# Two alternating chains of exponential steps on VectorE, with 72 instead of 67 tiles

## The chip, the cores and the metric

The kernel runs on one core of one Trainium2 chip. The metric is the device time of one execution in microseconds. Each time is the median of several executions; the profile is of one execution.

## The reference

Attention with a soft cap over 8 batches and 12 heads, 448 tokens, head size 64, and behind it a soft mixture of 8 experts with 4 slots each:

```python
scores = scale * np.matmul(q, k.transpose(0, 1, 3, 2))
scores = cap * np.tanh(scores / cap)                 # cap = 30
scores = scores - np.max(scores, axis=-1, keepdims=True)
attn = np.exp(scores)
attn = attn / (np.sum(attn, axis=-1, keepdims=True) + 1e-09)
x = np.matmul(attn, v)                               # heads side by side: (3584, 768)

logits = x @ phi                                     # (3584, 32)
d = softmax over tokens of logits; slot_input = d.T @ x
slot_out[e] = np.maximum(slot_input[e] @ w1[e], 0.0) @ w2[e]
c = softmax over slots of logits; out = c @ slot_out
```

## The kernel before

The 96 heads are taken as 48 pairs. A pair's scores stand transposed, keys on the partitions: a *tile* is 64 keys of each of the two heads on 128 partitions, with 448 queries along the free axis, so a pair has 7 tiles and the whole work 336. Six tiles make a *chunk*; there are 56 chunks, and the main loop's iteration `j` works on chunk `j`. The loop's pattern repeats every seven iterations: 42 tiles, six pairs, the twelve heads of one batch.

For each half chunk (three tiles) TensorE writes scores to one of two PSUM buffers `sc` (`qk_chunk`, line 316), and ScalarE takes tanh into the chunk's buffer `ex` as f16 (`tanh_chunk`, line 325). The exponential of `cap` times that is then made in place, as bf16. For most tiles ScalarE does it (`exp_chunk`, line 329, one instruction a chunk). The first `taken(j)` tiles of some chunks go to VectorE instead, where `poly_exp` makes the exponential in eight steps: a power of two by scaling into the exponent's bits and a polynomial of the third degree for the rest. Steps 0, 1, 2, 4 and 7 (lines 369, 371, 372, 374 and 377) have one tensor as input; steps 3, 5 and 6 (lines 373, 375, 376) have two. Steps 1 to 6 use the work buffers `xf` and `xp`; steps 0, 6 and 7 write into the tile itself. There is one `xf` and one `xp`, each two tiles wide, so a chain of a chunk has to be past step 6 before the next chain's step 1.

Two iterations after a pair's last tile was scored, TensorE multiplies its seven tiles by the values (`pv_first`, `pv_tail`, `pv_rest`, line 395) into the one PSUM buffer `pv`; VectorE then takes the reciprocal of the sums (line 402) and scales (line 405). VectorE also copies transposed keys, queries and outputs out of PSUM (`kT` and `qT` at line 278, `xT` at line 457). GpSimd casts the values of the next pairs to bf16 (`vcast`, line 286, behind the PV that used the buffer), copies the small exponentials `e` of the mixture (line 488, after ScalarE made them at line 482), and issues the DMAs that load queries and keys (line 186) and the experts' weights (lines 117 and 121). SyncE issues the loads of the values.

The order on each engine is written out by hand (`manual_schedule`): an instruction stands where Python issues it. An iteration runs named slots in a fixed order, `0`, `m`, `e`, `a`, `b`, `r`, `c`, `d`, each with a part `<` ahead and a part `>` behind, and side work is put into them with `at(j, slot, ...)`. Between them stand the tanh of both halves (ahead of `m` and `e`), the exponential of chunk `j - 1` and the first part of PV (between `e` and `a`), the scores of the next chunk (ahead of `b`, and between `c` and `d`), and the rest of PV with its reciprocal and scaling (between `b` and `c`).

Which chunks VectorE takes tiles of, and where each of the eight steps stands, are the tables `SHARE` (by `j % 7`: chunk's tiles, then for each step the distance in iterations and the slot) and `EDGE` (for the first and last chunks). After the attention come the last pairs, the experts' two layers (lines 845 and 878) and the outputs (lines 914, 918, 961, 968, 970).

Of the kernel before, what the change touches and what calls it, by code (L numbers as in the profile page):

```python
# [12 lines left out]
U16 = mybir.dt.uint16  # L13
F16 = mybir.dt.float16
# [4 lines left out]
P = 128  # L19
# [3 lines left out]
S = 448  # L23
# [14 lines left out]
def kernel(  # L38
# [27 lines left out]
    NCH = NTILE // CH  # L66
# [66 lines left out]

    att = ExitStack()
    ld = att.enter_context(tc.tile_pool(name="ld", bufs=1))
    NP = 2
    homes = {}
    for nm in ("qk0", "ex1", "wk", "ldv", "ex2", "ex3", "vb0", "qk1", "ex4", "ex0", "vb1"):
        homes[nm] = att.enter_context(tc.tile_pool(name=nm, bufs=1))
# [1 line left out]
    vb = [homes["vb0"], homes["vb1"]]  # L141
    qk = [homes["qk0"], homes["qk1"]]
    ldv, wk = homes["ldv"], homes["wk"]
    xf = wk.tile([P, NP * S], U16, name="xf")
    xp = wk.tile([P, NP * S], F16, name="xp")
    xs = att.enter_context(tc.tile_pool(name="xs", bufs=4))
    attp = ExitStack()
    psS = attp.enter_context(tc.tile_pool(name="psS", bufs=2, space=PSUM))
    psV = attp.enter_context(tc.tile_pool(name="psV", bufs=1, space=PSUM))
# [181 lines left out]
    def exp_chunk(j):  # L331
# [1 line left out]

    SHARE = {0: (2, ((0, "<b"), (0, ">d"), (1, ">a"), (1, ">a"), (1, ">b"), (1, ">d"), (1, ">d"), (2, ">a"))),
# [4 lines left out]
    EDGE = {3: (1, ((0, ">b"), (0, ">b"), (0, "<c"), (0, ">c"), (0, ">d"), (1, ">a"), (1, ">a"), (1, "<b"))),  # L341
# [7 lines left out]
    shared = {j: SHARE[j % 7] for j in range(3, NCH - 2)  # L349
              if j % 7 in SHARE and j + SHARE[j % 7][1][-1][0] < NCH - 1}  # L350
    shared.update(EDGE)

    octaves = cap * math.log2(math.e)
    base = math.ceil(octaves) + 1
    if base + octaves > 127:
        shared = {}

    def taken(j):
        return shared[j][0] if j in shared else 0
# [4 lines left out]
    def poly_exp(j, tiles, n):  # L364
        n1 = tiles * S
        t = exs[j][:, 0:tiles, :].rearrange("p u s -> p (u s)")
        y, f, p = t.bitcast(U16), xf[:, 0:n1], xp[:, 0:n1]
        steps = (
            lambda: dve.tensor_scalar(y, t.bitcast(F16), octaves * STEP, base * STEP + c0,  # L369
                                      ALU.mult, ALU.add),  # L370
            lambda: dve.tensor_scalar(f, y, STEP - 1, None, ALU.bitwise_and),  # L371
            lambda: dve.tensor_scalar(p, f, c3, c2, ALU.mult, ALU.add),  # L372
            lambda: dve.tensor_tensor(p, p, f, op=ALU.mult),  # L373
            lambda: dve.tensor_scalar(p, p, c1, None, ALU.add),  # L374
            lambda: dve.tensor_tensor(p, p, f, op=ALU.mult),  # L375
            lambda: dve.tensor_tensor(y, y, p, op=ALU.add),  # L376
            lambda: dve.tensor_scalar(y, y, 128.0 / STEP, 128.0 * (127 - base),
                                      ALU.mult, ALU.add))
        steps[n]()
# [173 lines left out]
    def at(j, slot, f, *a):  # L553
        if j < 0:
            j, slot = 0, "b"
        aux.setdefault((j, slot), []).append((f, a))
# [21 lines left out]
    for b in range(B):  # L578
        j, p = b * PER, 6 * b

        def when(nm):
            return j + WHEN[nm][0], WHEN[nm][1]
# [17 lines left out]
        if b < B - 1:  # L600
# [5 lines left out]
                at(*when("en"), e_norm, b)  # L606
            if b % 2:
                at(*when("es"), e_sums, b // 2)
    for j, (tiles, places) in shared.items():
        for n, (dj, slot) in enumerate(places):  # L610
            at(j + dj, slot, poly_exp, j, tiles, n)
    for n, job in enumerate(wjobs):
        at(1 + n * (NCH - 5) // len(wjobs), "b", *job)
    for j, slot, n in ((0, "a", 10), (0, "c", 10), (1, "b", 10), (1, "c", 8)):
# [207 lines left out]
    for n0, half in sorted(w2_spilled, key=lambda x: (x[1], x[0])):  # L822
        t = tl.tile([P, 4, HD], BF16, name=f"w2t{n0}_{half}")
# [123 lines left out]
    for n in range(B // 2 * NT):  # L947
        bb, c = divmod(n, NT)
# [15 lines left out]
        if n == NH or c == 0 or full:  # L964
            ob, n1 = wts.tile([P, 2, 2, HD], F32, name="ob", tag="w1", bufs=E), n
# [44 lines left out]
```

## Time and profile before

| | |
|---|---|
| median of 3 runs | 296.27 us (295.21 to 296.57) |
| span of the profiled execution | 293.9 us, first to last instruction |
| mean granted TensorE clock | 0.985 |
| time of the profiled execution itself | not given; by the three runs 1.3 to 2.7 us lie outside the span |
| exponential on ScalarE (line 329) | 58 instructions, 119.5 us busy |
| tanh on ScalarE (line 325) | 113 instructions, 147.5 us busy |
| steps of `poly_exp` on VectorE | 28 chains of two tiles, 11 of one; 312 of VectorE's 554 instructions |

Engines: PE is TensorE's matmul, PEld its weight load, DVE VectorE, ACT ScalarE, POOL GpSimd, SP SyncE. A line of a timeline gives the start and the duration in us, the engine, the line of the kernel, the operation, the output and input tiles with their shapes, and how many instructions it stands for; in brackets the idle time ahead and what ended it. A busy engine isn't an engine at its best: an instruction that is held by another engine counts as busy, and neighbours that don't depend on each other overlap a little, so that the time from one start to the next is what an instruction costs.

### The profile page before, as it was taken

What the parts mean: (1) busy time and instruction counts of PE and PEld (TensorE: products, weight loads), DVE (VectorE), ACT (ScalarE), POOL (GpSimd) and SP (SyncE); (2) the same over time, 40 slices, a digit from 0 to 9 for tenths busy, and PEclk for the clock granted to TensorE, in tenths of its full rate; (3) what the DMA queues carried; (4) which work ended last, traced back from release to release, by engine and by line L of the source; (5) the groups of instructions that cost most, each with busy time, mean ns of one, the idle gap of its engine ahead of it and who ended that gap; (6) DMA issues with size and microseconds to landing.
All of it is one profiled execution on the core that took longest, in us unless ns stands there. A gap on an engine that the chain in (4) does not pass through costs nothing.

```text
span 293.9 us, 10870 instructions
## 1 busy us (share of the span) xinstructions
PE 255.4 (87%) x4728; PEld 173.9 (59%) x4728; DVE 240.4 (82%) x554; ACT 260.3 (89%) x211; POOL 138.2 (47%) x200
## 2 busy tenths in 40 slices
PE   8898889998999899979988998899989899998620
PEld 6655556756675667556756675667566668542300
DVE  3728998999999999999999989999999976246740
ACT  4999999999999999999999999999999997237620
POOL 4593554763676367635673658365643220300000
PEclk9999999999999999999999999999999999999985
DMA  7999999999999999999999999999999567989896
GB/s 273 217 194 206 221 176 212 203 191 218 230 218 193 210 228 224 199 208 227 189 179 217 223 217 184 216 229 228 209 191 219 131 216 237 407 321 376 323 427 287
DMA packets 58561, 68.13 MB, mean 232 GB/s; under 512 B 4241, under 2 KB 54673, under 8 KB 58513
## 3 DMA queue, kind: packets, MB, share of 16 engines
q0 software_dynamic: 42448, 35.31, 77.8%
q1 hardware_dynamic: 15776, 31.89, 30.8%
q8 instruction: 37, 0.61, 0.8%
q10 hardware_dynamic: 288, 0.23, 0.2%
q14 instruction: 12, 0.09, 0.1%
HBM read 91.72 MB, written 19.27 MB: 378 GB/s over the span
## 4 chain that ended last, share of the span: by engine, by line
PE 35%; DVE 32%; ACT 21%; issue 4%; DMA 2%; POOL 2%; DVEq 0%; SPq 0%; ACTq 0%
PE pv L395 12%; ACT ex L325 11%; ACT ex L329 9%; PE sc L316 6%; DVE xq L405 4%; DVE ex L376 3%; DVE xp L375 3%; DVE xp L373 3%; DVE xf L371 2%; DVE xp L372 2%; DVE ex L369 2%; DVE kT L278 2%; DVE xp L374 2%; DVE qT L278 2%; PE so_ps L878 2%
## 5 line engine op out<-in xcount | busy, mean ns | idle before, releaser
L325 ACT ACTIVATE ex<-sc 128x1344 f16<-128x1344 f32 (+1 forms) x113 | 147.5, 1410 | 1.7 <-PE sc L316 1.6
L329 ACT ACTIVATE ex<-ex 128x1792 bf16<-128x1792 f16 (+5 forms) x58 | 119.5, 2064 | 0.1
L395 PE MATMUL pv<-vbd,ex 128*128 128x130 bf16 (+1 forms) x1610 | 94.4, 211 | 6.2 <-POOL vbd L286 2.7
L395 PEld LDWEIGHTS <-ex 128*128 128x128 bf16 (+1 forms) x1680 | 75.7, 101 | 34.1 <-PE sc L316 9.2
L316 PE MATMUL sc<-qT,kT 64*64 64x448 bf16 x672 | 70.5, 359 | 4.0 <-ACT ex L325 1.6
L286 POOL CAST vbd<-vraw 64x896 bf16<-64x896 f32 x46 | 44.1, 959 | 52.8 <-PE pv L395 37.3
L316 PEld LDWEIGHTS <-kT 64*64 64x64 bf16 x672 | 24.5, 105 | 10.0 <-issue 5.8
L405 DVE TENSOR_TENSOR xq<-pv,rec 128x448 bf16<-128x448 f32 x46 | 28.7, 624 | 1.6
L117 POOL DMA_DIRECT2D w1b<-in_moe_w_dram x32 | 24.9, 781 | 0.0
L488 POOL COPY e<-E 128x512 bf16<-128x512 bf16 x9 | 6.3, 705 | 37.4 <-PE eps L507 19.9
L376 DVE TENSOR_TENSOR ex<-ex,xp 128x896 uint16<-128x896 uint16 (+1 forms) x39 | 21.8, 559 | 1.2
L294 POOL MEMSET vbd<- 64x1 bf16 x22 | 3.0, 136 | 41.1 <-PE pv L395 41.1
L375 DVE TENSOR_TENSOR xp<-xp,xf 128x896 f16<-128x896 f16 (+1 forms) x39 | 22.0, 563 | 0.4
L373 DVE TENSOR_TENSOR xp<-xp,xf 128x896 f16<-128x896 f16 (+1 forms) x39 | 21.6, 554 | 0.7
L276 PE MATMUL qps<-ident,qb 128*64 128x128 bf16 x308 | 12.8, 221 | 8.5 <-DVE kT L278 6.6
L278 DVE COPY kT<-kps 128x896 bf16<-128x896 bf16 x23 | 14.3, 622 | 6.1 <-PE kps L276 5.7
L276 PEld LDWEIGHTS <-qb 128*64 128x64 bf16 x308 | 10.9, 109 | 13.7 <-issue 13.2
L425 PE MATMUL pv<-ones 128*128 128x57 bf16 x474 | 18.6, 188 | 0.0
L372 DVE TENSOR_SCALAR xp<-xf 128x896 f16<-128x896 uint16 (+1 forms) x39 | 17.8, 456 | 0.5
L186 POOL DMA_DIRECT2D qb<-in_q_dram x22 | 16.7, 759 | 3.0 <-DMA kraw<-in_k_dram 3.0
L371 DVE TENSOR_SCALAR xf<-ex 128x896 uint16<-128x896 uint16 (+1 forms) x39 | 17.3, 444 | 0.3
L457 DVE COPY xT<-xps 128x896 bf16<-128x896 bf16 (+1 forms) x24 | 14.4, 600 | 3.0 <-PE xps L448 2.5
(135 smaller groups left out, 365.5 us busy)
## 6 DMA issues: line engine op xcount, KB each, us to landing
w1b<-in_moe_w_dram POOLq DMA_DIRECT2D x32, 384.0 KB, 8.6
vraw<-in_v_dram SPq DMA_DIRECT2D x44, 224.0 KB, 6.1
w2d<-in_moe_w_dram POOLq DMA_DIRECT2D x21, 384.0 KB, 9.5
w2t<-w2d SPq DMA_DIRECT2D x21, 384.0 KB, 7.2
out_dram<-ob SPq DMA_DIRECT2D x7, 768.0 KB, 7.6
qb<-in_q_dram POOLq DMA_DIRECT2D x22, 224.0 KB, 7.3
kb<-in_k_dram POOLq DMA_DIRECT2D x22, 224.0 KB, 6.2
out_dram<-obh SPq DMA_DIRECT2D x23, 192.0 KB, 2.0
```

Of the source, the lines that this page charges most:

```text
L117: pool.dma_start(out=w1b[e][:, js, fs], in_=w1r[:, e, js, fs])
L276: pe.transpose(ps[h * HP:h * HP + HP, c, :], src[:, h, c * DH:(c + 1) * DH], ident)
L278: dve.tensor_copy(t, ps)
L286: pool.tensor_copy(vbds[Q % 2][r, :, :, c0:c0 + DH], raw[r])
L316: pe.matmul(sc[cs, u, 0:S], qkT["k", Q][r, c, cs], qkT["q", Q][r, :, cs], start=True, stop=True)
L325: act.activation(exs[j][:, half * CS + u0:half * CS + u1, :].bitcast(F16), sc[:, u0:u1, 0:S], ACT.Tanh, scale=qk_scale / cap)
L329: act.activation(exs[j][:, u0:u1, :], exs[j][:, u0:u1, :].bitcast(F16), ACT.Exp, scale=cap)
L373: lambda: dve.tensor_tensor(p, p, f, op=ALU.mult),
L375: lambda: dve.tensor_tensor(p, p, f, op=ALU.mult),
L376: lambda: dve.tensor_tensor(y, y, p, op=ALU.add),
L395: pe.matmul(out_, exs[j][r, u, q0:q0 + (HP if tail else P)], v_, start=(c == 0 and g == gs[0] < NF), stop=(c == NT - 1), skip_group_check= ...
L405: dve.tensor_tensor(xq[Q][:, h, s0:s1, :], pv[:, 0:s1 - s0, 0:DH], rec.to_broadcast([P, s1 - s0, DH]), op=ALU.mult)
```

## The change

There are now two work buffers `xf` and two `xp`: number 0 two tiles wide in the old place, number 1 one tile wide in a new pool behind the others. `SHARED` says for each chunk how many of its tiles VectorE takes and which buffers they use, and `POLY` gives for each place in the loop the steps that stand there, in order, as (chunk, step). Chains with buffer 0 take two tiles (in chunk 6 one), chains with buffer 1 take one, and a chain on one buffer may run between the steps of a chain on the other. In a period of seven chunks VectorE takes 2, 1, 2, 1, 2, 0, 2 tiles (by `j % 7` from 0) instead of 2, 0, 2, 0, 2, 2, 1. In all there are 27 chains of two tiles and 18 of one: 72 tiles instead of 67. The arithmetic of a step is as before. Line numbers behind the tables grow by 225; the steps 0 to 7 stand at lines 594 to 602.

```diff
-    NP = 2
...
-    xf = wk.tile([P, NP * S], U16, name="xf")
-    xp = wk.tile([P, NP * S], F16, name="xp")
     xs = att.enter_context(tc.tile_pool(name="xs", bufs=4))
+    more = att.enter_context(tc.tile_pool(name="more", bufs=1))
+    room = tuple(enumerate(zip((wk, more), (2, 1))))
+    xf = [home.tile([P, n * S], U16, name=f"xf{x}") for x, (home, n) in room]
+    xp = [home.tile([P, n * S], F16, name=f"xp{x}") for x, (home, n) in room]
...
-    SHARE = {0: (2, ((0, "<b"), (0, ">d"), (1, ">a"), (1, ">a"), (1, ">b"), (1, ">d"), (1, ">d"), (2, ">a"))),
-             2: (2, ((0, ">b"), (0, "<c"), (1, ">a"), (1, "<b"), (1, "<b"), (2, "e"), (2, ">a"), (2, "<b"))),
-             4: (2, ((0, ">a"), (0, ">b"), (0, "<c"), (0, ">d"), (0, ">d"), (1, ">a"), (1, "<b"), (1, ">c"))),
-             5: (2, ((0, "<d"), (0, "<d"), (1, ">a"), (1, ">a"), (1, "<c"), (1, "<d"), (1, "<d"), (2, "e"))),
-             6: (1, ((0, "e"), (0, ">d"), (0, ">d"), (1, ">a"), (1, ">a"), (1, ">c"), (1, "<d"), (2, "<b")))}
-    EDGE = {3: (1, ((0, ">b"), (0, ">b"), (0, "<c"), (0, ">c"), (0, ">d"), (1, ">a"), (1, ">a"), (1, "<b"))),
...
-    shared.update(EDGE)
+    SHARED = {3: (1, 1), 4: (2, 0), 5: (1, 1), 6: (1, 0), 7: (2, 0), 8: (1, 1), 9: (2, 0), 10: (1, 1),
+              11: (2, 0), 13: (2, 0), 14: (2, 0), 15: (1, 1), 16: (2, 0), 17: (1, 1), 18: (2, 0), 20: (2, 0),
...
+    POLY = {(3, 'e'): ((3, 0),),
...
+            (16, 'e'): ((15, 4),),
+            (16, '>a'): ((14, 7),),
+            (16, '>b'): ((15, 5), (16, 0)),
+            (16, '<c'): ((16, 1),),
+            (16, '>d'): ((16, 2), (15, 6)),
+            (17, 'e'): ((16, 3), (17, 0), (16, 4), (15, 7)),
+            (17, '>a'): ((17, 1),),
+            (17, '<c'): ((17, 2),),
+            (17, '>d'): ((17, 3),),
+            (18, 'e'): ((16, 5),),
+            (18, '>a'): ((18, 0), (16, 6), (16, 7)),
+            (18, '>b'): ((18, 1), (17, 4)),
+            (18, '<c'): ((18, 2),),
+            (18, '>d'): ((18, 3), (17, 5), (18, 4)),
+            (19, '>a'): ((18, 5),),
+            (19, '>d'): ((18, 6),),
+            (20, 'e'): ((18, 7),),
+            (20, '>a'): ((20, 0),),
+            (20, '>b'): ((17, 6),),
+            (20, '<c'): ((17, 7),),
+            (20, '>c'): ((20, 1),),
+            (20, '>d'): ((20, 2), (20, 3), (20, 4)),
...
+            (55, 'e'): ((54, 3), (54, 4), (54, 5), (54, 6), (54, 7))}
+    shared = dict(SHARED)
...
-        y, f, p = t.bitcast(U16), xf[:, 0:n1], xp[:, 0:n1]
+        x = shared[j][1]
+        y, f, p = t.bitcast(U16), xf[x][:, 0:n1], xp[x][:, 0:n1]
...
-    for j, (tiles, places) in shared.items():
-        for n, (dj, slot) in enumerate(places):
-            at(j + dj, slot, poly_exp, j, tiles, n)
+    for (j, slot), ops in POLY.items():
+        for chunk, n in ops:
+            at(j, slot, poly_exp, chunk, shared[chunk][0], n)
```

More of the change, by code (lines that the diff above doesn't have):

```diff
@@ L332, in exp_chunk @@
         exp_part(j, taken(j), CH)
-    SHARE = {0: (2, ((0, "<b"), (0, ">d"), (1, ">a"), (1, ">a"), (1, ">b"), (1, ">d"), (1, ">d"), (2, ">a"))),
[4 rows of a table removed]
-    EDGE = {3: (1, ((0, ">b"), (0, ">b"), (0, "<c"), (0, ">c"), (0, ">d"), (1, ">a"), (1, ">a"), (1, "<b"))),
[7 rows of a table removed]
-    shared = {j: SHARE[j % 7] for j in range(3, NCH - 2)
-              if j % 7 in SHARE and j + SHARE[j % 7][1][-1][0] < NCH - 1}
-    shared.update(EDGE)
+    SHARED = {3: (1, 1), 4: (2, 0), 5: (1, 1), 6: (1, 0), 7: (2, 0), 8: (1, 1), 9: (2, 0), 10: (1, 1),
[5 rows of a table added]
@@ L355 @@
     if base + octaves > 127:
-        shared = {}
+        shared, POLY = {}, {}
     def taken(j):
```

208 lines of the change are left out of this document (added), and 11 rows, old and new, of tables (EDGE, SHARED).

## The prediction

> **What bounds the kernel now.** I read the busy times, then the windows by stage, then ScalarE's timeline, and last VectorE's beside GpSimd's.
>
> ```profile
> PE 255.4 (87%) x4728; PEld 173.9 (59%) x4728; DVE 240.4 (82%) x554; ACT 260.3 (89%) x211; POOL 138.2 (47%) x200
> ```
> ```profile
> 83.00:112.50 29.50, 27.38 (x554) 19.34 (x552) 27.96 (x66) 29.50 (x23) 17.93 (x25) 1.00 1.19 212
> 172.50:202.00 29.50, 27.17 (x547) 19.12 (x545) 27.87 (x64) 29.50 (x23) 17.72 (x25) 1.00 1.22 211
> ```
> The whole-span shares hide the attention stage. In a window there (length, then busy time of PE, PEld, DVE, ACT, POOL) ScalarE is busy for all of its 29.50 us, VectorE for 27.96 of them. So from 6.6 to about 237 us ScalarE sets the pace, and VectorE follows within 5%. TensorE's clock is 1.00 there.
>
> ```profile
> 105.39 2.57 ACT L329 ACTIVATE ex<-ex 128x2688 bf16<-128x2688 f16 x1
> 107.73 2.60 ACT L325 ACTIVATE ex<-sc 128x1344 f16<-128x1344 f32 x2
> 110.07 1.84 ACT L329 ACTIVATE ex<-ex 128x1792 bf16<-128x1792 f16 x1
> 111.66 1.44 ACT L325 ACTIVATE ex<-sc 128x1344 f16<-128x1344 f32 x1
> ```
> Neighbours overlap, so the cost of an instruction is start to start: 2.34 us for the exponential of six tiles (105.39 to 107.73), 1.59 for four, so 0.373 us a tile; 1.17 for a tanh.
>
> ```profile
> 64.60 0.63 DVE L373 TENSOR_TENSOR xp<-xp,xf 128x896 f16<-128x896 f16 x1
> 65.26 0.39 DVE L374 TENSOR_SCALAR xp<-xp 128x896 f16<-128x896 f16 x1
> 65.69 0.62 DVE L375 TENSOR_TENSOR xp<-xp,xf 128x896 f16<-128x896 f16 x1
> 66.35 0.63 DVE L376 TENSOR_TENSOR ex<-ex,xp 128x896 uint16<-128x896 uint16 x1
> 66.89 0.62 DVE L278 COPY kT<-kps 128x896 bf16<-128x896 bf16 x1
> 67.43 0.27 DVE L371 TENSOR_SCALAR xf<-ex 128x448 uint16<-128x448 uint16 x1
> 67.73 0.28 DVE L372 TENSOR_SCALAR xp<-xf 128x448 f16<-128x448 uint16 x1
> 67.92 0.39 DVE L377 TENSOR_SCALAR ex<-ex 128x896 uint16<-128x896 uint16 x1
> 68.22 0.62 DVE L278 COPY qT<-qps 128x896 bf16<-128x896 bf16 x1
> ```
> Two neighbouring steps of one chain stand 0.66 us apart after a two-input step on two tiles (64.60 to 65.26, 65.69 to 66.35) and 0.43 after a fast (one-input) step; before work of another kind it is 0.54 (66.35 to 66.89) and 0.30 (67.92 to 68.22). So a step that reads its neighbour's result costs some 0.115 us more. On one tile: 0.19 fast (67.73 to 67.92), 0.31 two-input.
>
> ```profile
> 111.29 0.95 POOL L286 CAST vbd<-vraw 64x896 bf16<-64x896 f32 x1
> 112.04 0.68 DVE L375 TENSOR_TENSOR xp<-xp,xf 128x896 f16<-128x896 f16 x1
> 113.39 0.75 POOL L488 COPY e<-E 128x512 bf16<-128x512 bf16 x1 [1.15 <-ACT E L482]
> 113.59 0.80 DVE L377 TENSOR_SCALAR ex<-ex 128x896 uint16<-128x896 uint16 x1
> 114.84 0.76 POOL L117 DMA_DIRECT2D w1b<-in_moe_w_dram  x1
> 115.10 0.72 DVE L371 TENSOR_SCALAR xf<-ex 128x896 uint16<-128x896 uint16 x1
> ```
> A fast step that starts inside a GpSimd copy or cast ends 0.2 us after it (114.39 against 114.14): 0.80 us instead of 0.39. One that starts 0.24 us or more into GpSimd's issue of a DMA waits for its end too (115.82 against 115.60). Over the whole stage 55 of the 195 fast steps are held, by 13.4 us together; 2.0 us in each steady period.
>
> **The change, part by part.** GpSimd's, SyncE's and TensorE's instructions stand in the same order before and after; only ScalarE's sizes and VectorE's order change. The span is 293.9 us; the three timed runs are 295.2 to 296.6, so 1.3 to 2.7 us lie outside it; I add differences to the median, 296.27.
>
> The loop repeats every seven chunks. Between the starts of the small exponential (line 482) at 53.50 and 231.82 lie six periods of 29.72 us on average. ScalarE's own work in one is 14 x 1.17 + (4 x 1.587 + 1.958 + 2 x 2.334) + 0.155 = 29.51. With 2, 1, 2, 1, 2, 0, 2 tiles taken (10 instead of 9) the bracket is 4 x 1.587 + 2 x 1.958 + 2.334 = 12.60 instead of 12.97, and the work 29.14. Five tiles in all are 1.87 us: six in the periods, one fewer at the ends.
>
> VectorE, start to start: a two-tile chain is 5 x 0.30 + 3 x 0.54 = 3.12, a one-tile chain 5 x 0.19 + 3 x 0.31 = 1.88. A period has four and one of them now, four and two afterwards: +1.88. In the order of instructions, neighbouring steps of one chain, where the second reads the first's result, fall from 16 to 8 a period (127 to 77 in all): -0.92. Net +0.96. (All of it: one two-tile chain less, seven one-tile chains more, +10.0; 50 fewer such neighbours, -5.8; +4.3.) The rest of a period (nine copies out of PSUM at 0.54, six norms at 0.78, small ones) does not change. So VectorE's work without holds goes from 26.4 to 27.36 us. Of the 29.72, 26.4 is work, 2.0 is holds, and 1.3 is waiting, 0.5 of it labelled (kT for kps, rec for pv).
>
> So with unchanged holds VectorE needs 27.36 + 2.0 = 29.36 us a period, more than ScalarE's 29.14: it becomes the bound. How much the holds change, the trace of before can't show. From below: 0.41 of the 2.0 is the row at 113.59, which the new order replaces (in `18, '>a'` the two-input step 6 now stands where the copy of e runs, step 7 behind it), so 1.6; with the other casts dodged as well, 1.3. From above: fast steps go from 25 to 30 a period, and at the same rate holds are 2.4. I take 2.2, nearer the upper end, since most holds come from DMA issues, which the new order does not move. Of the 1.3 us of waiting I leave 0.25, since a late VectorE finds its inputs ready. 27.36 + 2.2 + 0.25 = 29.8, against 29.72: +0.1 x 6 = +0.6, and +0.37 for the tile that ScalarE gets back at the ends: +0.9 us, 297.2.
>
> Does a two-input step dodge a copy? The row at 112.04 says no: it starts 0.20 us before the cast's end and takes 0.68 instead of 0.62, as a fast step in that position does (0.45 instead of 0.39), while no row starts one deep inside. The Trainium skill ("SBUF — State Buffer", section "SBUF: two separate sides") calls the port that VectorE and GpSimd share an exclusive lock, which also a VectorE step with two SBUF inputs needs against a GpSimd operation that reads SBUF; this trace agrees at that one position (+0.06 us), and by that rule the 0.41 us isn't won.
>
> Against the second chain stands another rule. The Trainium skill ("VectorE: DVE Perf Modes", section "The DRAIN you can't avoid") says that a semaphore between VectorE operations costs nothing and that only their number counts. By it the alternation would win none of the 5.8 us. The rows disagree: of the two-input step at line 373, 18 with their reader next stand 0.655 us from it on average, 10 with other work between 0.55.
>
> The rest costs nothing. The new buffers come last in the pool, so no later tile changes places; the 21 reloads of w2t behind it start at the same waits. PV reads tiles later than their last step in program order in every case; the closest case (same iteration, step 7 in slot a, read in the second half of PV) is no closer than in the kernel before, where no PV wait names these steps.
>
> **The rivals.** One, ScalarE stays the bound: holds fall to 1.3 and VectorE, 27.36 + 1.3 + 0.25 = 28.9, fits under 29.14. With the 0.2 us that ScalarE loses now, a period is 29.34: -0.38 x 6 + 0.37 = -1.9, so 294.4. For it: a fast step right before the copy of e (`(18, 0)`) starts ahead of it and isn't held. Against: only some holds are casts. It decides once holds are under 1.5 us.
>
> Two, the other side: a one-tile step is caught by a whole cast. `18, '>b'` puts `(17, 4)` behind `(18, 1)`; that place is 115.73 in the period shown, and GpSimd's next cast starts at 115.59 and ends at 116.60. Held to its end the step costs 0.9 us more, the reciprocal and norm behind it are late, and TensorE's next PV waits for that one pv buffer. Against: a step that starts just ahead of a cast isn't held. If half the periods' worth lands, 29.8 + 0.5 = 30.3: +0.55 x 6 + 0.37 = +3.6, so 299.9; in every period 302. It decides from +0.2 us a period.
>
> Three, alternation wins nothing (the semaphore rule above): +0.92 x 6 = +5.5 on the forecast, 302.7. The rows speak against it; I count it with the second.
>
> **How the numbers follow.** VectorE takes over near break-even: 0.42, 295.6 to 298.8. ScalarE stays: 0.34, 293.2 to 295.3. Holds grow: 0.24, 298 and up. A measurement of this kernel tells about 0.5% from no change, 1.48 us. Faster by more is most of the second case (0.28). Slower by more is a third of the first and nearly all of the third (0.36). The rest is 0.36. The range is 293.8 to 300.5; about 0.17 lies outside.
>
> **What the profile afterwards would show.** Right: periods between the small exponentials of 29.7 to 29.9 us, tanh or exponential on ScalarE waiting for scores, VectorE without the labelled waits for kps and pv. ScalarE's rival: periods of 29.3 and ScalarE still busy throughout. The other side: 30 us and more, and a one-tile step of about 1 us beside a cast. Wrong at the root: one-tile steps that don't cost 0.19 and 0.31, or neighbours of different chains that stand 0.66 apart.

## The result, and the profile after

The changed kernel takes 294.12 us (median of 16 runs, 293.56 to 296.97) against 295.91 for the kernel before (16 runs): ratio 0.9945, 95% interval 0.9925 to 0.9966. It is faster by just over half a per cent, 3.1 us under the forecast of 297.2 and close to the 294.4 of rival one. (The forecast was added to 296.27, the median of the first three runs of the kernel before.) The span of its profiled execution, the fastest of the 16, is 291.8 us, 2.1 less than before; by the medians the gain is 1.8.

From the page of the profile after: the busy times, the engines of the chain that ended last, and two groups (busy time, mean ns, then the idle time ahead and what ended most of it).

```profile
PE 254.9 (87%) x4728; PEld 171.4 (59%) x4728; DVE 239.4 (82%) x602; ACT 259.0 (89%) x211; POOL 138.2 (47%) x200
...
DVE 39%; PE 30%; ACT 17%; issue 6%; DMA 2%; POOL 1%; DVEq 0%; SPq 0%; ACTq 0%
...
L620 PE MATMUL pv<-vbd,ex 128*128 128x130 bf16 (+1 forms) x1610 | 96.7, 212 | 13.4 <-DVE ex L602 6.6
L620 PEld LDWEIGHTS <-ex 128*128 128x128 bf16 (+1 forms) x1680 | 75.8, 101 | 43.9 <-DVE ex L602 10.2
```

VectorE makes 48 instructions more and yet is busy for 1.0 us less. In the chain it now leads with 39% (before: PE 35%, DVE 32%, ACT 21%). TensorE's multiplication by the values waits for step 7 of `poly_exp` (`ex L602`), 6.6 us in 16 waits; in the kernel before its matmuls there waited mostly for the cast `vbd` (2.7 us) and never for step 7.

The windows by stage, columns as before:

```profile
82.95:112.45 29.50, 27.60 (x557) 19.21 (x556) 28.33 (x74) 29.38 (x23) 18.14 (x25) 1.00 1.17 208
171.53:201.03 29.50, 27.25 (x548) 18.89 (x546) 28.34 (x73) 29.50 (x24) 17.82 (x25) 1.00 1.25 216
```

VectorE's busy time of 28.3 us contains eight or nine instructions more than before, and far less holding. To size the holds I compare each fast step with its duration when nothing is in its way (0.385 us on two tiles, 0.275 on one). Between the first and the last small exponential 47 of 152 fast steps were held before, for 2.05 us a period; afterwards it is 26 of 175, for 0.83. Both kinds fell: holds by DMA issues from 1.28 to 0.49 us a period, by copies and casts from 0.77 to 0.35. All of this 0.35 is the copy of `e`: no cast holds a fast step any more. Two-input steps are held for 0.26 us a period (before 0.05), by casts and in one period by the copy.

The small exponentials (line 707) start at 53.41, 82.95, 112.56, 142.01, 171.53, 200.97 and 231.01: periods of 29.54, 29.61, 29.45, 29.52, 29.44 and 30.04, mean 29.60 (before 29.72). The sixth holds 33 tiles on ScalarE and the others 32, because VectorE now takes none of chunk 50; before, all six hold 33. At 0.373 us that tile is most of what the sixth is longer by. The five full periods are 29.51 on average, and the same five before 29.74. Here is the timeline of VectorE, GpSimd and ScalarE at the start of one period:

```profile
112.66 0.62 DVE L600 TENSOR_TENSOR xp<-xp,xf 128x896 f16<-128x896 f16 x1
113.04 0.71 POOL L713 COPY e<-E 128x512 bf16<-128x512 bf16 x1 [0.94 <-ACT E L707]
113.20 0.80 DVE L594 TENSOR_SCALAR ex<-ex 128x896 uint16<-128x896 f16 x1
113.70 0.74 POOL L187 DMA_DIRECT2D kb<-in_k_dram  x1
113.92 0.61 DVE L601 TENSOR_TENSOR ex<-ex,xp 128x896 uint16<-128x896 uint16 x1
114.44 0.76 POOL L117 DMA_DIRECT2D w1b<-in_moe_w_dram  x1
114.57 0.39 DVE L602 TENSOR_SCALAR ex<-ex 128x896 uint16<-128x896 uint16 x1
114.88 0.61 DVE L279 COPY kT<-kps 128x896 bf16<-128x896 bf16 x1
115.41 0.38 DVE L596 TENSOR_SCALAR xf<-ex 128x896 uint16<-128x896 uint16 x1
115.71 0.27 DVE L599 TENSOR_SCALAR xp<-xp 128x448 f16<-128x448 f16 x1
115.98 0.92 POOL L287 CAST vbd<-vraw 64x896 bf16<-64x896 f32 x1 [0.78 <-PE pv L620]
115.98 0.20 DVE L627 RECIPROCAL rec<-pv 128x7 f32<-128x7 f32 x1
115.84 2.64 ACT L326 ACTIVATE ex<-sc 128x1344 f16<-128x1344 f32 x2
118.38 1.69 ACT L330 ACTIVATE ex<-ex 128x1792 bf16<-128x1792 f16 x1
119.96 2.56 ACT L326 ACTIVATE ex<-sc 128x1344 f16<-128x1344 f32 x2
122.42 2.44 ACT L330 ACTIVATE ex<-ex 128x2688 bf16<-128x2688 f16 x1
```

Step 0 at 113.20 starts inside the copy of `e` and takes 0.80 us, held for 0.42. So it is in five of the six periods; in the other the two-input step 6 starts 0.14 us into the copy (at 172.46) and takes 1.03 us. Steps 6 and 7 behind it meet GpSimd's two DMA issues and are not held: the two-input step runs across an issue in 0.61, and the fast step at 114.57 starts 0.13 us into the next issue. The one-tile step 4 at 115.71, rival two's step, starts 0.27 us ahead of the cast and takes its usual 0.27. ScalarE's two tanh at 115.84 cover 2.54 us instead of 2.34, because the scores for the second end only at 117.14. In each of the six periods ScalarE loses time at this place, 0.16 to 0.34 us, and 0.10 or so at the two tanh at 119.96; from one start to the next everywhere else it keeps its own pace, but for 0.08 once. The way to this place is the same each time. PV starts 0.06 us behind the end of step 7 (the row at 114.57), the scores queued behind that PV end 2.19 us behind step 7, and the tanh starts 0.04 us later. In the kernel before, the scores for this tanh were done 0.9 us or more before ScalarE came to it.

A third of the gain in the span lies behind the six periods. ScalarE's timeline of the last stretch, first of the kernel before, then after:

```profile
235.12 1.49 ACT L325 ACTIVATE ex<-sc 128x1344 f16<-128x1344 f32 x1
236.96 1.29 ACT L325 ACTIVATE ex<-sc 128x1344 f16<-128x1344 f32 x1 [0.35 <-PE sc L316]
...
244.41 2.63 ACT L329 ACTIVATE ex<-ex 128x1344 bf16<-128x1344 f16 x3
```
```profile
234.31 2.47 ACT L326 ACTIVATE ex<-sc 128x1344 f16<-128x1344 f32 x2
236.65 2.09 ACT L330 ACTIVATE ex<-ex 128x2240 bf16<-128x2240 f16 x1
...
242.91 2.66 ACT L330 ACTIVATE ex<-ex 128x1344 bf16<-128x1344 f16 x3
```

Before, the second of these tanh waits for its scores and stands 1.84 us behind the first instead of 1.17; after, it doesn't wait, and the two take 2.34 from start to start. From the last small exponential to the first of the last three big ones it is 12.59 us before and 11.90 after, with the same tiles on ScalarE. What made the scores late before stands ahead of them, on VectorE and GpSimd (first the kernel before, then after):

```profile
230.56 1.11 POOL L286 CAST vbd<-vraw 64x896 bf16<-64x896 f32 x1
230.78 1.03 DVE L371 TENSOR_SCALAR xf<-ex 128x448 uint16<-128x448 uint16 x1
231.73 0.18 DVE L402 RECIPROCAL rec<-pv 128x7 f32<-128x7 f32 x1
```
```profile
229.75 1.11 POOL L287 CAST vbd<-vraw 64x896 bf16<-64x896 f32 x1
229.97 0.20 DVE L627 RECIPROCAL rec<-pv 128x7 f32<-128x7 f32 x1
```

A one-tile step 1 started 0.22 us into a whole cast and was held for 0.75 us, with the reciprocal, the next PV and its scores behind it. The new order has no one-tile step there, and the reciprocal comes 0.22 us behind the start of the cast instead of 1.17. The 2.1 us of span are 0.09 ahead of the first period, 6 x 0.12 = 0.72 in the periods, 0.69 in the last stretch and 0.6 behind it. The last is within what one execution differs from another: from the first of those three exponentials to the end the kernels with the new tables take between 48.9 and 49.7 us, those with the old between 49.4 and 49.6.

### The profile page after: what moved, and what is told of

The parts are those of the page before. It is cut to its first block, busy times and chain, and to the rows that moved or that the text cites. A ratio compares the mean times of both kernels' runs of the same rounds, so it can differ in the third digit from the quotient of the medians.

```text
span 291.8 us, 10919 instructions
## 1 busy us (share of the span) xinstructions
PE 254.9 (87%) x4728; PEld 171.4 (59%) x4728; DVE 239.4 (82%) x602; ACT 259.0 (89%) x211; POOL 138.2 (47%) x200
## 4 chain that ended last, share of the span: by engine, by line
DVE 39%; PE 30%; ACT 17%; issue 6%; DMA 2%; POOL 1%; DVEq 0%; SPq 0%; ACTq 0%
PE pv L620 9%; ACT ex L326 8%; ACT ex L330 8%; DVE xq L630 6%; DVE ex L601 4%; DVE xp L598 4%; PE sc L317 4%; DVE xT L682 4%; DVE xp L600 3%; DVE ex L594 3%; DVE ex L602 2%; DVE xp L597 2%; PE qps L277 2%; DVE xf L596 2%; PE pv L650 2%
## 5 line engine op out<-in xcount | busy, mean ns | idle before, releaser
L326 ACT ACTIVATE ex<-sc 128x1344 f16<-128x1344 f32 (+1 forms) x113 | 142.8, 1316 | 1.4 <-PE sc L317 1.2
L330 ACT ACTIVATE ex<-ex 128x1792 bf16<-128x1792 f16 (+5 forms) x58 | 112.3, 1942 | 0.1
L620 PE MATMUL pv<-vbd,ex 128*128 128x130 bf16 (+1 forms) x1610 | 96.7, 212 | 13.4 <-DVE ex L602 6.6
L598 DVE TENSOR_TENSOR xp<-xp,xf 128x896 f16<-128x896 f16 (+1 forms) x45 | 24.3, 539 | 0.6
L601 DVE TENSOR_TENSOR ex<-ex,xp 128x896 uint16<-128x896 uint16 (+1 forms) x45 | 24.2, 537 | 0.2
L600 DVE TENSOR_TENSOR xp<-xp,xf 128x896 f16<-128x896 f16 (+1 forms) x45 | 23.5, 522 | 0.3
L594 DVE TENSOR_SCALAR ex<-ex 128x896 uint16<-128x896 f16 (+1 forms) x45 | 19.0, 422 | 0.0
L599 DVE TENSOR_SCALAR xp<-xp 128x896 f16<-128x896 f16 (+1 forms) x45 | 16.3, 363 | 0.4
L597 DVE TENSOR_SCALAR xp<-xf 128x896 f16<-128x896 uint16 (+1 forms) x45 | 16.0, 356 | 0.3
L121 POOL DMA_DIRECT2D w2d<-in_moe_w_dram x21 | 16.3, 787 | 0.0
L279 DVE COPY qT<-qps 128x896 bf16<-128x896 bf16 x23 | 14.2, 620 | 2.4 <-PE qps L277 1.6
```

The source lines that it names most:

```text
L279: dve.tensor_copy(t, ps)
L326: act.activation(exs[j][:, half * CS + u0:half * CS + u1, :].bitcast(F16), sc[:, u0:u1, 0:S], ACT.Tanh, scale=qk_scale / cap)
L330: act.activation(exs[j][:, u0:u1, :], exs[j][:, u0:u1, :].bitcast(F16), ACT.Exp, scale=cap)
L620: pe.matmul(out_, exs[j][r, u, q0:q0 + (HP if tail else P)], v_, start=(c == 0 and g == gs[0] < NF), stop=(c == NT - 1), skip_group_check= ...
```

## The experiments

Each ratio is to the kernel before, measured beside it; 1% is 2.96 us. Two kernels are compared by the difference of their ratios and by their periods.

**One tile more, one buffer.** From the kernel before:

```diff
-             6: (1, ((0, "e"), ...
+             6: (2, ((0, "e"), ...
```

> The kernel before, with two tiles instead of one in the sixth chunk of each period (73 tiles, one buffer, steps where they were). ScalarE's work falls by 0.37 us a period, VectorE's grows by 3.12 - 1.88 = 1.24. Theory (VectorE is nearly full, and the change pays only because its holds fell from 2.05 to 1.1 us a period): VectorE needs 26.4 + 1.24 + 2.05 = 29.7 us and some waiting, periods of 29.9 to 30.3, 1 to 3 us slower than before (ratio 1.003 to 1.010). Rival (ScalarE alone sets the pace, the tiles are the gain): 2.2 us faster, ratio 0.992.

310.2 us, ratio 1.0473 (1.0413 to 1.0533), far beyond what was expected. The periods are 31.41, 31.40, 32.45, 31.90, 31.52 and 29.63; the sixth, which has no added tile, is as before. Holds are 2.4 us a period; the rest is lost as follows, here in the second period (VectorE, GpSimd and ScalarE, timeline):

```profile
103.53 1.15 POOL L286 CAST vbd<-vraw 64x896 bf16<-64x896 f32 x1 [3.77 <-PE pv L395]
103.81 1.12 DVE L369 TENSOR_SCALAR ex<-ex 128x896 uint16<-128x896 f16 x1
104.86 0.19 DVE L402 RECIPROCAL rec<-pv 128x7 f32<-128x7 f32 x1
107.85 1.29 ACT L325 ACTIVATE ex<-sc 128x1344 f16<-128x1344 f32 x1 [0.71 <-PE sc L316]
110.31 1.29 ACT L325 ACTIVATE ex<-sc 128x1344 f16<-128x1344 f32 x1 [1.17 <-PE sc L316]
```

Step 0 starts inside a cast and costs 0.74 us more; the reciprocal behind it is late, TensorE's next PV waits for the one `pv` buffer, and the scores queued behind that PV come late to ScalarE, which waits 0.71 and 1.17 us. In each of the five periods with the added tile ScalarE loses 2.1 to 2.7 us around this place. This is rival two's chain, at another step; how the added tile brings that step into the cast was not followed. Six tiles more without the new order lose 14 us.

**The new order without the tiles.** From the kernel after; the chains of one tile of chunks 10, 17, ..., 45 are left to ScalarE, so 66 tiles remain on VectorE:

```diff
+    dropped = {10, 17, 24, 31, 38, 45}
+    SHARED = {c: x for c, x in SHARED.items() if c not in dropped}
+    POLY = {at_: tuple(o for o in ops if o[0] not in dropped) for at_, ops in POLY.items()}
```

> The changed kernel without the one-tile chains of chunks 10, 17, 24, 31, 38 and 45: 66 tiles, new buffers and places. ScalarE's work is 29.51 us a period again, VectorE's 27.36 - 1.88 = 25.5. Theory (both engines within half a microsecond of the period): ScalarE is the bound without waits, periods of 29.55, about 0.5 us faster than before (ratio 0.997 to 1.000) and 1 us slower than the changed kernel. Rival (the fewer holds are the whole gain, the tiles bring nothing): as fast as the changed kernel or faster, ratio 0.994 or less.

295.29 us, ratio 0.9975 (0.9939 to 1.0011), periods of 29.67 on average. The first five are 29.60, 0.09 above ScalarE's own 29.51, and the sixth has a tile more on ScalarE (30.00): ScalarE sets the pace, and the order alone is worth next to nothing there. The timeline of VectorE and GpSimd has the row that the prediction lacked, a two-input step deep inside a copy:

```profile
113.73 0.61 POOL L716 COPY e<-E 128x512 bf16<-128x512 bf16 x1 [1.15 <-ACT E L710]
113.78 1.04 DVE L604 TENSOR_TENSOR ex<-ex,xp 128x896 uint16<-128x896 uint16 x1
```

It takes 1.04 us instead of 0.62 and is held for 0.42, as long as a fast step would be: a two-input step is no way around a copy. The Trainium skill ("SBUF — State Buffer", section "SBUF: two separate sides") calls the port that VectorE and GpSimd share an exclusive lock, which a VectorE operation with two SBUF inputs needs as well, against a GpSimd operation that reads SBUF; this row, deep inside the copy, agrees.

**More neighbours of one chain.** From the kernel after; within each place of the table the steps are sorted by chain, so 103 instead of 77 neighbours depend on each other, with the same steps and tiles:

```diff
+    POLY = {at_: tuple(sorted(ops)) for at_, ops in POLY.items()}
```

> The changed kernel, with the steps of each place in the loop sorted by chunk, so that 103 instead of 77 neighbours are one chain's: 26 x 0.115 = 3.0 us more on VectorE. Theory (a neighbour costs 0.115 us and VectorE is on the path for most of the period): 1 to 3 us slower than the changed kernel, ratio to before 0.998 to 1.005. Rival (the semaphore between neighbours costs nothing, or VectorE has room): as the changed kernel, 0.994.

295.89 us, ratio 1.0011 (0.9975 to 1.0046), 0.66% or 2.0 us above the kernel after; periods 29.91, which is 6 x 0.31 = 1.9 us. At 0.115 us a neighbour 26 of them would be 3.0. So alternation has a price near what the rows gave. The Trainium skill's rule that a semaphore costs nothing between VectorE operations ("VectorE: DVE Perf Modes", section "The DRAIN you can't avoid") would have put this run level with the kernel after; here the measurement decides against it. (Sorting also moves steps against GpSimd: holds are 1.20 us a period instead of 1.09, 0.7 us in six, so the 2.0 us are not all the neighbours'.)

**The copy of `e` moved behind the crowded place.** From the kernel after; `e_rep` is no longer called at the end of `e_exp`, in slot `m`, but behind slot `c` of the same iteration, after the cast:

```diff
-        e_rep(b)
...
+            at(j + 11, ">c", e_rep, b)
```

> The changed kernel, with GpSimd's copy of the small exponentials issued behind the fifth chunk's cast of values instead of ahead of it. In the changed kernel a fast step (chunk 25, step 0) is held 0.42 us by that copy, steps 6 and 7 of chunk 23 come late, PV waits for step 7 and the scores behind PV reach ScalarE 0.2 us late. Theory (this chain sets the period): ScalarE's gap in that iteration goes, 0.2 to 0.3 us a period, 1.2 to 2 us faster than the changed kernel, ratio 0.988 to 0.991. Rival (the hold is hidden, or the next hold takes its place): as the changed kernel, 0.994.

292.41 us, ratio 0.9863 (0.9817 to 0.9909): it beats both kernels. Periods are 29.36 on average, 0.22 to 0.26 shorter than each of the kernel after. Without the copy there, GpSimd's issues come earlier, and one of weights now meets step 0 (GpSimd and VectorE, timeline):

```profile
112.26 0.76 POOL L117 DMA_DIRECT2D w1b<-in_moe_w_dram  x1
112.69 0.56 DVE L594 TENSOR_SCALAR ex<-ex 128x896 uint16<-128x896 f16 x1
```

Step 0 is held for 0.13 to 0.17 us instead of 0.42, step 7 ends 0.24 to 0.28 us earlier behind the small exponential, and the loss at the tanh behind it falls from 0.16 to 0.34 us to 0.09 at most. All holds together hardly change, 0.99 us a period instead of 1.09: the copy in its new place holds two other steps, for 0.07 and 0.14 us, and the periods show nothing of it. The engines of the chain that ended last, from the page of this kernel:

```profile
ACT 39%; DVE 27%; PE 19%; issue 8%; DMA 2%; POOL 1%; DVEq 0%; SPq 0%; ACTq 0%
```

ScalarE leads again. The five full periods are 29.28 on average, near rival one's 29.34: ScalarE's own 29.14 and 0.14 lost.

**The same move in the kernel before:**

> The kernel before, with GpSimd's copy of the small exponentials issued behind the fifth chunk's cast, as in e4; nothing else. It takes a hold of 0.41 us a period from a step 7 that PV reads. Theory (before, VectorE had room and ScalarE lost only 0.2 us a period): at most 0.2 x 6 = 1.3 us faster, ratio 0.996 to 1.000. Rival (a late copy is worth 1.8 us by itself, whatever the schedule): ratio 0.994 or less, and then the tiles and chains brought less than they seem to.

295.7 us, ratio 0.9984 (0.9955 to 1.0013). In the kernel before, holds fall by 0.6 us a period (2.10 to 1.50), the 0.41 of step 7 among them, and the periods by 0.04 (29.72 to 29.68): taking holds away gains nothing where ScalarE sets the pace.

**The copy made twice.** From the kernel after:

```diff
+        for _ in range(2 if b < B - 2 else 1):
             pool.tensor_copy(e4s[b]...
```

> The changed kernel, with GpSimd's copy of the small exponentials made twice in a row in the six periods, so that the hold there is 0.4 + 0.6 to 0.7 us. Theory (the hold passes through step 7, PV and scores to ScalarE): each period 0.5 to 0.8 us longer, 3 to 5 us slower than the changed kernel, ratio to before 1.004 to 1.012. Rival (there is cover for it): ratio 0.9945 to 0.997.

298.88 us, ratio 1.0073 (1.0036 to 1.011). Step 6 is now held as well, for 0.40 us. The first three periods are 29.97, 30.04 and 29.88: each 0.43 longer than in the kernel after. Step 7 ends 0.43 us later, and the tanh behind it starts as much later. A hold of 0.40 us ahead of this step 7 passes into the period whole. (The later periods are worse, 31.08 and 31.79 among them; in one, fast steps are held for 2.4 us.)

**The late copy without the tiles** (the two edits above together):

> e4 (the late copy) without the six one-tile chains of e2: 66 tiles. ScalarE's work is 29.51 us a period instead of 29.14. Theory (with the late copy ScalarE is the bound, and each tile is worth its 0.37 us): periods of 29.5 to 29.6, 2.2 us slower than e4, ratio to before 0.993 to 0.995. Rival (the late copy and the places are the whole gain): as e4, 0.986.

294.95 us, ratio 0.996 (0.9925 to 0.9995), periods 29.67, the same as with the order alone. Against the late copy with all tiles it is 0.31 us a period, 1.9 in six; by ScalarE's 0.373 us a tile it would be 2.2. So a tile taken from ScalarE is worth nearly its full price, once VectorE has room for it; in the kernel after, with the hold, six tiles bring 6 x 0.07 = 0.4 us in the periods.

**Step 7 ahead of the next chain.** From the kernel after; in `>a` of chunks 11, 18, ..., 46 steps 6 and 7 stand ahead of step 0:

```diff
+    for c in range(11, 47, 7):
+        POLY[c, '>a'] = ((c - 2, 6), (c - 2, 7), (c, 0))
```

> The changed kernel, with steps 6 and 7 of the chain in hand put ahead of the next chain's step 0 beside GpSimd's copy of the small exponentials (the place behind a in the fifth iteration of a period). The two-input step 6 now starts inside the copy and should be held by it to its end, some 0.4 us, as step 0 was; step 7 comes about 0.25 us earlier than in the changed kernel. Theory (what counts is when step 7 is done, since PV waits for it and the scores stand behind PV): 0.5 to 1.5 us faster than the changed kernel, ratio to before 0.989 to 0.993. Rival (what counts is how long VectorE is held in all): as the changed kernel, 0.9945, or slower for the six added neighbours of one chain.

296.21 us, ratio 0.9985 (0.9957 to 1.0014). The first two periods gain (29.36 and 29.44), the next three lose (30.03, 30.48, 30.28). VectorE, GpSimd and ScalarE in the third, timeline:

```profile
115.41 0.92 POOL L287 CAST vbd<-vraw 64x896 bf16<-64x896 f32 x1 [0.47 <-PE pv L622]
115.44 1.03 DVE L601 TENSOR_SCALAR xp<-xp 128x448 f16<-128x448 f16 x1
116.39 0.19 DVE L629 RECIPROCAL rec<-pv 128x7 f32<-128x7 f32 x1
121.53 1.29 ACT L326 ACTIVATE ex<-sc 128x1344 f16<-128x1344 f32 x1 [0.63 <-PE sc L317]
```

This is rival two to the letter: the one-tile step 4 of `18, '>b'` starts 0.03 us into the cast, takes 1.03 instead of 0.27, and ScalarE waits 0.63 for scores.

**That step moved away.** The same, and:

```diff
+        POLY[c, '>b'], POLY[c, '<c'] = ((c, 1),), ((c, 2), (c - 1, 4))
```

> e5 with the one-tile chain's step 4 in the fifth iteration of a period moved from the place ahead of the reciprocal to behind the norm. In e5 that step started 0.03 us behind the start of a whole cast in the later periods and was held 0.76 us, the norm came late and PV waited for the pv buffer. Theory (that one hold is what made e5 slower than the changed kernel; without it an earlier step 7 pays): periods of 29.3 to 29.5 throughout, as e5's first two, 1.5 to 3 us faster than e5, ratio to before 0.988 to 0.993. Rival (e5 is slower for its six added neighbours and for the order as such): as e5, 0.997 to 1.000.

293.16 us, ratio 0.9883 (0.9848 to 0.9918): 3.0 us won back by one step's place, and 1.8 us faster than the kernel after. Five periods are 29.2 to 29.8. In the fourth, 30.28, holds are 2.1 us, 0.64 of them a step 2 that starts 0.43 us into a cast of 1.2 us (at 145.59).

**Both mends together**, the late copy and the moved step:

> e4 (late copy) with the same step 4 moved behind the norm. In e4 it stood 0.33 us ahead of the cast and was not held. Theory (ScalarE is the bound there, 0.1 to 0.2 us a period lost): within 0.5 us of e4, ratio to before 0.986 to 0.990. Rival (VectorE's lateness still sets the pace, and a norm that is 0.19 us earlier pays in each period): 1 us or more faster than e4.

Not as expected: 295.97 us, ratio 0.9971 (0.9946 to 0.9997), 3.2 us slower than the late copy alone, with periods of 29.78 to 29.98 and one of 30.32. VectorE and GpSimd, timeline:

```profile
117.67 0.76 POOL L714 COPY e<-E 128x512 bf16<-128x512 bf16 x1
117.88 0.68 DVE L601 TENSOR_SCALAR xp<-xp 128x448 f16<-128x448 f16 x1
119.12 0.77 POOL L121 DMA_DIRECT2D w2d<-in_moe_w_dram  x1
119.58 0.53 DVE L601 TENSOR_SCALAR xp<-xp 128x896 f16<-128x896 f16 x1
```

The step moved away from the cast now starts inside the late copy (0.68 instead of 0.27), and the two-tile step 4 behind it falls into a DMA issue (0.53 instead of 0.39). A period is 0.58 us longer on average than with the late copy alone. Two edits that each won in another kernel fall on each other.

**More DMA issues on GpSimd**, one behind each of the 64 issues of weights, about one an iteration, small and read by nobody, once from the kernel after and once from the kernel before:

```diff
+    last = att.enter_context(tc.tile_pool(name="last", bufs=3))
...
+    def extra():
+        pool.dma_start(out=last.tile([P, NS], moe_phi.dtype, name="more_dma", tag="x"), in_=moe_phi[0:P, :])
...
         at(1 + n * (NCH - 5) // len(wjobs), "b", *job)
+        at(1 + n * (NCH - 5) // len(wjobs), "b", extra)
```

> The kernel after, with one small DMA issue more on GpSimd in each iteration (128 rows of 128 bytes, behind the weight issue), whose result nobody reads. It puts back holds by DMA issues, of which the kernel after has about 1 us a period less than the kernel before. The forecast's sum (VectorE is full, every microsecond of hold is a microsecond of the period): holds of h us more a period cost 6 x h; if fast-step holds go from 0.83 to 1.5 or 2.0 us a period, 298 to 301 us, periods of 30.3 to 30.8. My present theory (VectorE has about 1 us a period of waiting, and only holds ahead of a step 7 or a norm with a deadline count): less than half of that, 294.5 to 297, periods of 29.6 to 30.0, with ScalarE waiting only where a held step stands ahead of step 7 or of a norm.

From the kernel after: 298.95 us, ratio 1.0092 (1.0065 to 1.0119). Holds grow from 1.09 to 1.85 us a period, the period from 29.60 to 30.20, which is four fifths of it. I had expected under half, from a theory that VectorE's waiting would hide them; on average that is not so. Period by period the two don't go together: in the second, holds grow by 0.45 us and the period by 0.04, in the third by 0.58 and 0.67. Nor need all of it come from holds: the chain that ended last goes for 9% through DMAs here (2% in the kernel after), so GpSimd's own work is late as well. The fourth period, 31.50, is the worst; timeline of VectorE and GpSimd there:

```profile
150.21 1.00 POOL L288 CAST vbd<-vraw 64x896 bf16<-64x896 f32 x1
150.28 1.42 DVE L599 TENSOR_TENSOR xp<-xp,xf 128x896 f16<-128x896 f16 x1
```

A two-input step that starts 0.07 us into a cast is held for 0.80.

> The kernel before, with the same extra DMA issue on GpSimd in each iteration. The forecast's sum put 1.3 us of waiting into a period of the kernel before, ScalarE as the bound: holds up to 1 us more should cost under 0.2 us a period, 296 to 297 us. If instead holds count by their place, the kernel before, whose step 7 and norms have more slack, loses less than the kernel after does with the same edit, 296 to 298. If both lose the same, it is not VectorE's holds but GpSimd's own lateness (casts behind the extra issue) that costs.

From the kernel before: 297.86 us, ratio 1.0059 (1.0032 to 1.0086). Holds grow by 0.53 us a period (fast steps 2.05 to 2.46, two-input 0.05 to 0.17), and five of the six periods are 29.74 on average against 29.67 for the same five before: nearly nothing. The other takes 32.06; there GpSimd's issue of `qb` waits for earlier transfers, and VectorE waits 2.04 us in all, most of it for `kps` and `qps`. That is lateness of GpSimd itself; its cause stays open.

## Why the prediction failed

**The bound: right that VectorE delays ScalarE, wrong that the period is VectorE's sum.** The forecast said that VectorE takes over, and that a period is then its work, its holds and its waiting added up. VectorE does delay ScalarE. ScalarE's own work in the six periods is 29.20 us each (29.14, and a tile more in the sixth), they take 29.60, and nearly all of the difference is lost at the two places behind one step 7. The two experiments with the copy of `e` move just this: made twice, step 7 ends 0.43 us later in the first three periods, and each takes 0.43 more; moved, step 7 ends 0.24 us earlier or a little more and a period takes 0.22 to 0.26 less. But the holds in all are nearly the same with the late copy, 0.99 us a period against 1.09. So a hold counts by the step that it makes late, and the sum of the holds is no measure of the period. That VectorE leads the chain with 39% would not show it alone: in the kernel before, where taking holds away gains nothing, ScalarE has 21%.

**The size of the holds: the step that failed.** "I take 2.2, nearer the upper end, since most holds come from DMA issues, which the new order does not move." The issues did keep their order, but the steps moved against them. Holds of fast steps by issues alone fell from 1.28 to 0.49 us a period, and all of them together came to 0.83 + 0.26 = 1.09, which is below the lower end of 1.3. Scaling the old rate by the number of fast steps was no bound at all: a hold is a meeting of two places, and a new order makes new meetings. The one row that the forecast followed by hand came out at its size and at another step: the copy of `e` still costs 0.42 us, but it is step 0 that starts 0.15 to 0.32 us inside it in five of the six periods, where the forecast placed step 6 and rival one had step 0 start ahead.

**The waiting: also mis-sized, the other way.** The forecast left 0.25 us a period, "since a late VectorE finds its inputs ready". In a full period its work of 27.36 (by the rows' prices, not measured anew) and the holds, 1.13 there, leave 29.51 - 28.49 = 1.0 us. As it said, the waits for `kps` are gone from the six periods; but the reciprocal's waits for `pv` grew from 1.4 to 3.1 us in the six, and labelled waits are 0.55 us a period as before (0.53). This is no room for a hold ahead of step 7, as the doubled copy shows. Where VectorE waits for `pv`, it waits for a TensorE that waited for step 7 (6.6 us in 16 waits); that this explains the whole 1.0 us is argued and not shown. "No PV wait names these steps" was true of the kernel before, but for one wait of 0.2 us of a weight load, and of it alone. 27.36 + 2.2 + 0.25 = 29.8 should have read 27.36 + 1.13 + 1.0 = 29.5: errors of 1.1 and 0.75 us that for the most part cancel, so that the forecast of the period is as near as it is by luck.

**The ends: a term put at nothing.** The forecast's +0.37 for one tile is real, but the tile stands in the sixth measured period (30.04) and not at the ends, where ScalarE has 50 and 21 tiles both before and after. What the ends brought was 0.09 ahead and 0.69 in the last stretch, both gains, and the forecast had no term for either. In all ten kernels with the new tables the last stretch is 11.90 or 11.91 us, in the four with the old ones 12.59 or 12.60, whatever else was edited. The four all have a one-tile step of 1.03 us in the cast ahead of it (the row at 230.78), and none of the ten has. So the old order's last chunks (`EDGE`) held rival two's meeting already, in plain sight in the trace of before, and the new order removes it; no run moves that step alone.

Of the 3.1 us between the forecast (+0.97) and the span (-2.1), the six periods with that tile are 1.7 (+0.97 against -0.72), the ends 0.8, and 0.6 is what one execution differs from another.

**The neighbours: right.** Dependent neighbours still stand 0.66 us apart, work of the other chain 0.54, and 26 pairs more cost 2.0 us, up to 0.7 of it holds, where 3.0 were expected.

**Rival one named the time and not the mechanism.** Its condition, holds under 1.5 us, came true; its period of 29.34 did not (29.51), and the last stretch made up the difference, which is luck. The kernel with the late copy is near to rival one as written.

**Rival two is real and missed by 0.27 us.** In the profile shown, the one-tile step 4 starts that much ahead of the cast. Putting step 7 forward moves it to 0.03 us inside, and it then costs 0.76 us (0.9 forecast).

**Rival three is excluded** by the time, 8.6 us under its 302.7, and spoken against by the run with more neighbours of one chain.

## What to carry to other kernels

Where one engine holds another, don't price a new order by the old order's rate of holds: lay the new places of the steps beside the other engine's copies, casts and issues, and follow those that come closest, for 0.3 us decide. Then ask what waits for the step that is held: 0.25 us less ahead of a step 7 that PV waits for was worth a period 0.22 to 0.26 us shorter, while 0.2 us more at two other steps cost nothing that was seen. A period times its count leaves out the ends; their steps have to be followed like those in the middle, the old ones too. When two engines are as close as here, take the cheapest hold away from the one that makes the other late: moving one copy of 0.7 us won more (2.4 us) than the whole change.

## What the hardware showed

- A two-input step on VectorE that starts inside a GpSimd copy or cast is held like a fast one: 1.04 us instead of 0.62 beside a copy, 1.42 beside a cast.
- Such a step is not held by GpSimd's issue of a DMA: 0.61 us at 113.92 of the kernel after, across most of an issue. In the fourteen traces 623 two-input steps start inside an issue and touch no copy or cast; none of them is more than 0.01 us over its usual time.
- A fast step is held by an issue when it starts late enough in it (0.53 instead of 0.39 at 119.58 of the kernel with both mends, to 0.22 us past the issue's end). Of 181 that start less than 0.2 us into an issue none is held, as the one at 114.57 of the kernel after.
- A small DMA costs GpSimd nearly as much to issue as a large one: 0.63 us on average for 128 rows of 128 bytes, 0.77 for 384 KB (both in the kernel after with more issues).
